# Softmax sums stored in the factors' order, their transpose in the bank of the products with V, and the factors' first DMA issued by ScalarE

## The chip, the cores and the metric

The kernel runs on one NeuronCore of a Trainium2 chip. The metric is the device time of one execution in microseconds; several runs are made and their median is given. The profile is of one more execution of the same program, with its own time.

## What is computed

The reference is attention with a block-causal mask over 8 batches and 8 heads, a gated causal convolution, two dense layers, a two-dimensional Fourier mix and a feed-forward network. What the change touches is the softmax and what follows it:

```python
scores = np.where(mask, scores, -1000000000.0)
scores = scores - np.max(scores, axis=-1, keepdims=True)
attn = np.exp(scores)
attn = attn / (np.sum(attn, axis=-1, keepdims=True) + 1e-09)
return np.matmul(attn, v).astype(np.float32)
...
gate_pre += conv_w[k][None, None, :] * xp[:, k:k + S, :]
gate = 1.0 / (1.0 + np.exp(-gate_pre))
val = x @ w_val
return (gate * val @ w_out).astype(np.float32)
```

There are 8 batches, 8 heads of width 64 and 576 tokens; the kernel works on two heads at a time, so there are 32 pairs of heads, 4 to a batch.

## The kernel before

**Two phases.** `phase1` does the attention of all 32 pairs, with the convolution, the gating, the dense layers and the Fourier transform of each batch woven in as work for TensorE between the attention's steps. `phase2` is the feed-forward network over all tokens. The change is in `phase1`.

**One pair** has 9 units (`i` from 0 to 8): units 0 to 7 are blocks of 128 queries of the two heads by turns (even `i` head 0, odd `i` head 1), unit 8 holds the last 64 queries of both. The main loop counts units over all pairs (`n`), and each step of it emits different stages of different units: the scores `sc` on TensorE (`emit_qk`, L392), the row maximum `mx` on VectorE (`emit_max`), the exponential `PB` on ScalarE (`emit_exp`, L443), the transposes `pt` of `PB` on TensorE (`emit_t`, L490) and their copies out of PSUM, `PTa`, `PTb` and `PTc`, on ScalarE (L512), and at the pair's end the products with V, `av` and `ave` (`emit_av`, L517, matmuls at L535).

**The factors.** The exponential's accumulator leaves each query's sum in a column of the tile `su`: unit `i` writes column `i`, and unit 8, whose scores lie in two tiles, writes columns 8 and 9. `emit_recip` (L454) adds those two, adds 1e-9 and multiplies by 8, and takes three reciprocals into `re`, which re-order the columns: head 0's four blocks, the last block twice, head 1's four blocks. `emit_factors` (L468) transposes `re` on TensorE into a PSUM tile `rt` (L474), and a later stage copies it to SBUF on ScalarE (L479), stores it to a small buffer `f_d` in DRAM (L480) and reads it back by three DMAs that spread each head's factors over 64 partitions of the tile `XF` (L483). `scaled_x` (L548, L549) multiplies `av` and `ave` by `XF`. The rest of `finish_x` makes the high and low parts `XH`, `XL` and the convolution's taps `gate` (L564).

**What sets the order.** The loop's emission order and a scheduler in the framework, which orders each engine's instructions by readiness and priority. Stages that should come later are kept in `Chain` objects: `tick` runs one stage of each live chain per half step, and the list `tq` holds the evacuations of the two PSUM tiles of pool `ps_pt`, so that a new tile of that pool first runs the evacuation before the last. `rt` takes a tile of `ps_pt` before the change. The pool `ps_av` has one tile, `av`. SyncE (SP) issues every DMA of the kernel before the change, in one queue: the loads, the spreads `QQ`, `QD` and `K` of the split queries and keys, `f_d`, `XF` and the stores.

The names of the dense part on TensorE are `psv` (product with w_val), `psx`, `psy` and `pss` (product with w_out and the transforms), all made of matmuls at L165 to L167.

Of the kernel before, what the change touches and what calls it, by code (L numbers as in the profile page):

```python
# [8 lines left out]
F32 = mybir.dt.float32  # L9
F32R = mybir.dt.float32r  # L10
AF = mybir.ActivationFunctionType
ALU = mybir.AluOpType
# [5 lines left out]
def kernel(  # L18
# [13 lines left out]
    nc = tc.nc  # L32
    B, NP, P, S = q.shape
# [68 lines left out]
    def phase1():  # L102
        with ExitStack() as c1:
# [339 lines left out]
            def emit_exp(n):  # L443
                p, i = divmod(n, NB)
                if i == 0:

                    sums[p] = sm.tile([P, 12], F32, tag="su", name="su")
                su = sums[p]
                nm = maxs.pop(n)
                for j, (t, k0, w) in enumerate(scs.pop(n)):  # L450
                    nc.scalar.activation(out=PB[i][:, k0:k0 + w], in_=t, func=AF.Exp, bias=nm,  # L451
                                         accum_out=su[:, i + j:i + j + 1])

            def emit_recip(p):  # L454

                su = sums[p]
                re = sm.tile([P, 10], F32, tag="re", name="re")
                nc.vector.tensor_tensor(out=su[:, 8:9], in0=su[:, 8:9], in1=su[:, 9:10], op=ALU.add)

                nc.vector.tensor_scalar(out=su[:, 0:9], in0=su[:, 0:9], scalar1=1e-9, scalar2=8.0,  # L460
                                        op0=ALU.add, op1=ALU.mult)

                for h in range(2):
                    nc.vector.reciprocal(out=re[:, 6 * h:6 * h + 4], in_=su[:, h:8:2])
                nc.vector.reciprocal(out=re[:, 4:6], in_=su[:, 8:9].to_broadcast([P, 2]))
                recips[p] = re

            def emit_factors(p):  # L468

                re = recips.pop(p)  # L470
                if len(tq) > PTB - 1:
                    tq.pop(0).run()
                ps = ps_pt.tile([P, D], F32, tag="pt", name="rt")
                nc.tensor.transpose(ps[0:10, 0:P], re, ident)  # L474
                rt = sm.tile([P, P], F32, tag="rt", name="rt", bufs=2)
                to, fd = XFS[p % NXF], f_d[p % 2]

                def out():
                    nc.scalar.copy(out=rt[0:10], in_=ps[0:10, 0:P])  # L479
                    nc.sync.dma_start(out=fd, in_=rt[0:10])  # L480
                    row = fd.rearrange("c q -> (c q)").unsqueeze(0)
                    for h, at, n, c in ((0, 0, S, 0), (1, 768, 512, 0), (1, 704, 64, 512)):
                        nc.sync.dma_start(out=to[rs[h], c:c + n], in_=row[:, at:at + n].to_broadcast([64, n]))  # L483
                tq.append(Chain(out))

            tq = []
            VY = 3
            PTB = 2
# [27 lines left out]

            def emit_av(p):  # L517

                if p - 1 in fin:
                    fin[p - 1].run(1)  # L520
                t = ps_av.tile([P, D], F32, tag="av", name="av")
                if len(tq) > PTB - 1:
                    tq.pop(0).run()
# [353 lines left out]
            for n in range(NU + LT + LA):  # L877
# [18 lines left out]
                tick(old)  # L896
                advance(0, n, emit_max, 1)
                advance(1, n, emit_exp)
                old = list(live)
                if 0 <= n - LT < NU:  # L900
                    emit_t(n - LT)
                advance(0, n, emit_max)
                pr, ir = divmod(n - FR, NB)
                if n >= FR and pr < NPAIR:
                    if ir == 0:
                        emit_recip(pr)
                    if ir == 1:
                        emit_factors(pr)
                m = n - LT - LA
                if 0 <= m < NU:  # L910
                    pm, im = divmod(m, NB)
# [11 lines left out]
                            pend.append(dense(pm // NP))  # L923
                step(nst - nst // 2)
                tick(old)
            while pend:
                if not drain[0]:
                    drain[0] = 3
# [276 lines left out]
```

## Time and profile before

| what | value |
|---|---|
| median of 3 runs | 1521.37 us (1520.1 to 1521.79) |
| the profiled execution's own time | 1518.6 us |
| its span, first to last instruction | 1516.8 us |
| mean granted TensorE clock | 0.985 |
| TensorE busy | 1430.2 us (94%) |
| VectorE busy | 831.0 us (55%) |
| ScalarE busy | 648.1 us (43%) |
| GpSimd busy | 302.6 us (20%) |
| DMA queue of SP | 31.5% of 16 engines' span |

Phase 1 takes somewhat less than half the span and phase 2 the rest. The busy shares over the whole span mix the two; a share means something only inside one stage, which the rows further down give. An engine's wait is put down to the instruction that released it last.

### The profile page before, as it was taken

The numbers are of one execution on the slowest core, as the hardware profiler recorded it, in microseconds if no ns is written. First come the engines' busy times: TensorE is split into PE (matmuls) and PEld (weight loads), VectorE is DVE, ScalarE is ACT, GpSimd is POOL, SyncE is SP. The second block draws the span as 40 slices with busy tenths as digits, with TensorE's granted clock in tenths as the row PEclk, the third lists the DMA queues.
The fourth block names the chain that finished last, engine by engine and source line by source line (L and its number), as shares of the span: only waits on it lengthen the run. The fifth ranks groups of instructions, "written<-read, shape, count | busy, mean of one in ns | idle before, by whom it ended". The sixth has DMA issues, their size and how long they took to land.

```text
span 1516.8 us, 23187 instructions
## 1 busy us (share of the span) xinstructions
PE 1430.2 (94%) x8588; PEld 1207.8 (80%) x8588; DVE 831.0 (55%) x1712; ACT 648.1 (43%) x1642; POOL 302.6 (20%) x244
## 2 busy tenths in 40 slices
PE   5688999999999999998999999999999999999998
PEld 3466788888888888986677888888888888888887
DVE  5668687878787878689995223213223222322212
ACT  5577767676767686734452212112121211212110
POOL 2322232323232323122001111011111100111100
PEclk9699999999999999999999999999999999999999
DMA  7566565656565656133441010010101001010000
GB/s 208 150 158 200 132 176 158 167 138 173 137 176 137 176 132 173 46 135 126 168 140 56 0 56 1 1 55 0 56 0 56 1 10 46 1 56 0 29 0 28
DMA packets 122592, 138.75 MB, mean 91 GB/s; under 512 B 24112, under 2 KB 92016, under 8 KB 122480
## 3 DMA queue, kind: packets, MB, share of 16 engines
q1 hardware_dynamic: 122480, 137.27, 31.5%
q8 instruction: 68, 1.11, 0.3%
q14 instruction: 44, 0.36, 0.1%
HBM read 72.05 MB, written 19.04 MB: 60 GB/s over the span
## 4 chain that ended last, share of the span: by engine, by line
PE 50%; DVE 10%; issue 1%; POOL 0%; ACT 0%; DMA 0%; SPq 0%; DVEq 0%; POOLq 0%
PE o L1097 8%; PE psh L1079 8%; PE psh L1078 8%; PE psh L1077 8%; PE o L1095 8%; PE o L1096 8%; DVE st L74 1%; DVE st L76 1%; DVE st L84 1%; DVE st L72 1%; DVE W1L L989 1%; PE av L535 1%; DVE W2L L989 1%; DVE hl L1083 0%; PE pt L506 0%
## 5 line engine op out<-in xcount | busy, mean ns | idle before, releaser
L1083 DVE SCALAR_TENSOR_TENSOR hl<-psh,hh 128x512 fp32r<-128x512 f32 x144 | 99.4, 690 | 397.2 <-ACT hh L1082 397.1
L1082 ACT ACTIVATE hh<-psh 128x512 fp32r<-128x512 f32 x144 | 85.9, 597 | 510.7 <-PE psh L1079 510.7
L1097 PE MATMUL o<-hl,W2H 128*128 128x512 f32 x576 | 220.7, 394 | 13.2 <-DVE hl L1083 13.1
L1079 PE MATMUL psh<-UTH,W1L 128*128 128x512 f32 x576 | 225.4, 391 | 0.9 <-DVE W1L L989 0.9
L1077 PE MATMUL psh<-UTH,W1H 128*128 128x512 f32 x576 | 224.8, 391 | 0.8 <-ACT UTH L1042 0.8
L1078 PE MATMUL psh<-UTL,W1H 128*128 128x512 f32 x576 | 225.0, 391 | 0.4 <-DVE UTL L1043 0.4
L1095 PE MATMUL o<-hh,W2H 128*128 128x512 f32 x576 | 224.1, 389 | 0.0
L1096 PE MATMUL o<-hh,W2L 128*128 128x512 f32 x576 | 224.0, 389 | 0.0
L451 ACT ACTIVATE PB<-sc,mx 128x128 f32<-128x128 f32 (+4 forms) x320 | 165.6, 522 | 39.6 <-DVE mx L438 21.9
L506 PE MATMUL pt<-ident,PB 128*128 128x128 f32 x800 | 142.7, 284 | 17.7 <-ACT PTb L512 7.4
L1097 PEld LDWEIGHTS o<-hl,W2H 128*128 128x128 f32 x576 | 107.6, 189 | 40.9 <-DVE hl L1083 19.2
L506 PEld LDWEIGHTS pt<-ident,PB 128*128 128x128 f32 x800 | 100.4, 144 | 35.0 <-ACT PTb L512 13.5
L1077 PEld LDWEIGHTS psh<-UTH,W1H 128*128 128x128 f32 x576 | 108.6, 189 | 24.0 <-ACT UTH L1042 1.1
L1079 PEld LDWEIGHTS psh<-UTH,W1L 128*128 128x128 f32 x576 | 108.5, 188 | 24.0 <-DVE W1L L989 1.3
L1078 PEld LDWEIGHTS psh<-UTL,W1H 128*128 128x128 f32 x576 | 108.7, 189 | 23.6 <-DVE UTL L1043 0.9
L1095 PEld LDWEIGHTS o<-hh,W2H 128*128 128x128 f32 x576 | 108.1, 188 | 22.8 <-ACT hh L1082 0.2
L1096 PEld LDWEIGHTS o<-hh,W2L 128*128 128x128 f32 x576 | 108.1, 188 | 22.6
L564 DVE SCALAR_TENSOR_TENSOR gate<-XF,cw,gate 128x575 f32<-128x575 f32 (+3 forms) x128 | 123.5, 965 | 2.1 <-ACT gate L63 1.1
L1106 POOL TENSOR_TENSOR U<-o,U 128x512 f32<-128x512 f32 x32 | 40.3, 1290 | 364.8 <-DVE o L1104 364.8
L438 DVE TENSOR_REDUCE mx<-sc 128x1 f32<-128x384 f32 (+2 forms) x192 | 104.4, 561 | 4.9 <-PE sc L167 2.8
L406 PE MATMUL sc<-K,QQ 128*128 128x256 f32 (+2 forms) x256 | 88.6, 356 | 18.6 <-DMA QQ<-QHL 15.4
L560 POOL TENSOR_TENSOR XL<-XF,XH 128x576 fp32r<-128x576 f32 x32 | 45.6, 1426 | 276.7 <-ACT XH L57 268.9
(191 smaller groups left out, 2879.4 us busy)
## 6 DMA issues: line engine op xcount, KB each, us to landing
K<-KP SPq DMA_DIRECT2D x128, 144.0 KB, 2.6
QQ<-QHL SPq DMA_DIRECT2D x128, 128.0 KB, 3.5
rw<-in_w_ch SPq DMA_DIRECT2D x32, 512.0 KB, 4.2
VV<-in_v SPq DMA_DIRECT2D x32, 320.0 KB, 4.3
qraw<-in_q SPq DMA_DIRECT2D x32, 288.0 KB
kraw<-in_k SPq DMA_DIRECT2D x32, 288.0 KB, 5.9
out<-U SPq DMA_DIRECT2D x36, 256.0 KB, 2.0
QQ<-QHL SPq DMA_DIRECT2D x128, 64.0 KB, 2.0
```

The lines of the kernel that those rows point to most:

```text
L406: nc.tensor.matmul(t[:, o:o + w], q[:, 0, m], KK[p][h][:, 0:w], start=True, stop=False)
L438: nc.vector.reduce_max(out=mx[:, j:j + 1], in_=t, axis=AX.X, negate=one)
L451: nc.scalar.activation(out=PB[i][:, k0:k0 + w], in_=t, func=AF.Exp, bias=nm, accum_out=su[:, i + j:i + j + 1])
L506: nc.tensor.transpose(ps[:, j, :], PB[i][:, (j0 + j) * P:(j0 + j + 1) * P], ident)
L564: nc.vector.scalar_tensor_tensor(out=gate[c][:, s:S], in0=XF[:, 0:S - s], scalar=cw[:, c, 4 - s:5 - s], in1=gate[c][:, s:S], op0=ALU.mult, ...
L1077: nc.tensor.matmul(ps, W1H[f][:, c, :], UTH[g][:, c, :], start=(c == 0), stop=False)
L1078: nc.tensor.matmul(ps, W1H[f][:, c, :], UTL[g][:, c, :], start=False, stop=False)
L1079: nc.tensor.matmul(ps, W1L[f][:, c, :], UTH[g][:, c, :], start=False, stop=(c == 3))
L1083: nc.vector.scalar_tensor_tensor(out=l, in0=ps, scalar=0.0, in1=h.bitcast(F32), op0=ALU.max, op1=ALU.subtract)
L1095: nc.tensor.matmul(po[t], W2H[e][:, c], h, start=(e == 0), stop=False)
L1096: nc.tensor.matmul(po[t], W2L[e][:, c], h, start=False, stop=False)
L1097: nc.tensor.matmul(po[t], W2H[e][:, c], l, start=False, stop=(e == NF - 1))
```

## The change

The exponential's sums go straight into the factors' order: columns 0 to 3 head 0, 6 to 9 head 1, and 10 and 11 for unit 8; one add with two columns out makes columns 4 and 5. One reciprocal over ten columns takes the place of three. `emit_recip` is emitted earlier in its step and `emit_factors` at the end of its step. The transpose `rt` is put into the tile of `ps_av` in place of one of `ps_pt`, is no longer in `tq`, and its stage `out` is a chain of its own (`facs`), which `emit_av` runs at the latest. The evacuation of the pair before (`fin[p - 1].run(1)`) is forced in `emit_factors`, no longer in `emit_av`. The store to `f_d` is issued by ScalarE. The loads of `XF` stay with SP.

```diff
+                at = 10 if i == 8 else 6 * (i % 2) + i // 2
...
-                                         accum_out=su[:, i + j:i + j + 1])
+                                         accum_out=su[:, at + j:at + j + 1])
...
-                nc.vector.tensor_tensor(out=su[:, 8:9], in0=su[:, 8:9], in1=su[:, 9:10], op=ALU.add)
-
-                nc.vector.tensor_scalar(out=su[:, 0:9], in0=su[:, 0:9], scalar1=1e-9, scalar2=8.0,
+                nc.vector.tensor_tensor(out=su[:, 4:6], in0=su[:, 10:11].to_broadcast([P, 2]),
+                                        in1=su[:, 11:12].to_broadcast([P, 2]), op=ALU.add)
+
+                nc.vector.tensor_scalar(out=su[:, 0:10], in0=su[:, 0:10], scalar1=1e-9, scalar2=8.0,
                                         op0=ALU.add, op1=ALU.mult)
-                for h in range(2):
-                    nc.vector.reciprocal(out=re[:, 6 * h:6 * h + 4], in_=su[:, h:8:2])
-                nc.vector.reciprocal(out=re[:, 4:6], in_=su[:, 8:9].to_broadcast([P, 2]))
+                nc.vector.reciprocal(out=re, in_=su[:, 0:10])
...
-                if len(tq) > PTB - 1:
-                    tq.pop(0).run()
-                ps = ps_pt.tile([P, D], F32, tag="pt", name="rt")
+                if p - 1 in fin:
+                    fin[p - 1].run(1)
+                ps = ps_av.tile([P, D], F32, tag="av", name="rt")
...
-                    nc.sync.dma_start(out=fd, in_=rt[0:10])
+                    nc.scalar.dma_start(out=fd, in_=rt[0:10])
...
-                tq.append(Chain(out))
+                facs[p] = Chain(out)
...
-                if p - 1 in fin:
-                    fin[p - 1].run(1)
+                facs.pop(p).run()
...
+                pr, ir = divmod(n - FR, NB)
+                if n >= FR and pr < NPAIR and ir == 0:
+                    emit_recip(pr)
                 old = list(live)
...
-                pr, ir = divmod(n - FR, NB)
-                if n >= FR and pr < NPAIR:
-                    if ir == 0:
-                        emit_recip(pr)
-                    if ir == 1:
-                        emit_factors(pr)
...
                 tick(old)
+                if n >= FR and pr < NPAIR and ir == 1:
+                    emit_factors(pr)
```

Three places show what the scheduler makes of it. The first is TensorE's queue in the third pair of a batch (pair 18), once the batches follow one another steadily. `PB_123` and `PB_124` are the probabilities of units 5 and 6, `psx` is the product with w_out.

Before:

```order
L506 MATMUL pt<-ident,PB_123 128x128 x3
L474 MATMUL rt<-ident,re 10x128
L165 MATMUL psx<-GH_158,we_h 128x290
L166 MATMUL psx<-GL_162,we_h 128x290
L167 MATMUL psx<-GH_158,we_l 128x290
L165 MATMUL psx<-GH_159,we_h 128x290
L166 MATMUL psx<-GL_163,we_h 128x290
L167 MATMUL psx<-GH_159,we_l 128x290
L506 MATMUL pt<-ident,PB_124 128x128 x4
```

Now:

```order
L509 MATMUL pt<-ident,PB_123 128x128 x3
L165 MATMUL psx<-GH_158,we_h 128x290
L166 MATMUL psx<-GL_162,we_h 128x290
L167 MATMUL psx<-GH_158,we_l 128x290
L165 MATMUL psx<-GH_159,we_h 128x290
L166 MATMUL psx<-GL_163,we_h 128x290
L167 MATMUL psx<-GH_159,we_l 128x290
L475 MATMUL rt<-ident,re 10x128
L509 MATMUL pt<-ident,PB_124 128x128 x4
```

The transpose of the factors moved behind six matmuls, and nothing else moved. From pair 9 on every pair differs in this alone: in the first and second pair of a batch it moved behind two matmuls of `psv`, in the third behind six of `psx`, in the fourth behind six of `psy`. The number of matmuls is the same.

The second place is SP's queue in pair 1, among the first batches; `QQ_114` and `QQ_116` are the spread queries that the next pair's first scores read.

Before:

```order
L353 DMA QD_113<-QHL 64x2x64 x2
L480 DMA f_d_66<-rt 10x128
L377 DMA QQ_114<-QHL 64x2x256
L379 DMA QQ_114<-QHL 64x256
L377 DMA QQ_116<-QHL 64x2x256
L483 DMA XF_132<-f_d_66 64x576
L483 DMA XF_132<-f_d_66 64x512
L483 DMA XF_132<-f_d_66 64x64
L379 DMA QQ_116<-QHL 64x256
```

Now:

```order
L353 DMA QD_113<-QHL 64x2x64 x2
L485 DMA XF_132<-f_d_66 64x576
L485 DMA XF_132<-f_d_66 64x512
L485 DMA XF_132<-f_d_66 64x64
L377 DMA QQ_114<-QHL 64x2x256
L379 DMA QQ_114<-QHL 64x256
L377 DMA QQ_116<-QHL 64x2x256
```

The store left the queue, and the three loads of `XF` now stand ahead of the spreads `QQ`. So it is in pairs 0 to 7 (in pair 5 with one load between); from pair 8 on at least the first spreads stand ahead of `XF`.

The third place is TensorE's queue in pair 2, where `PB_124` to `PB_126` are units 6 to 8 of the pair and `K_559` or `K_557` the next pair's keys.

Before:

```order
L506 MATMUL pt<-ident,PB_123 128x128 x3
L406 MATMUL sc<-K_559,QQ_114 128x256
L407 MATMUL sc<-KL,QQ_114 128x256
L406 MATMUL sc<-K_559,QQ_114 128x256
L407 MATMUL sc<-KL,QQ_114 128x256
L474 MATMUL rt<-ident,re 10x128
L506 MATMUL pt<-ident,PB_124 128x128 x4
L506 MATMUL pt<-ident,PB_125 128x128 x4
```

Now:

```order
L509 MATMUL pt<-ident,PB_123 128x128 x3
L509 MATMUL pt<-ident,PB_124 128x128 x4
L509 MATMUL pt<-ident,PB_125 128x128 x4
L475 MATMUL rt<-ident,re 10x128
L509 MATMUL pt<-ident,PB_126 128x128 x5
L406 MATMUL sc<-K_557,QQ_114 128x256
L407 MATMUL sc<-KL,QQ_114 128x256
```

The next pair's first scores moved behind the transposes of units 6 to 8, and the factors' transpose stands among these. From the last pair's factors on, the rest of phase 1 and all of phase 2 stand in the same order on every engine as before.

## Rows read from the trace of the kernel before

**Rows 1.** Busy time by stretch of the span: PE, PEld, DVE, ACT, POOL, clock, DMA.

```profile
0.00:200.00 200.00, 154.06 (x1049) 118.62 (x1050) 135.86 (x316) 130.71 (x367) 55.24 (x65) 0.91 0.62 172
200.00:640.00 440.00, 421.99 (x3640) 384.40 (x3640) 348.37 (x874) 321.43 (x931) 126.55 (x92) 1.00 0.55 149
640.00:720.00 80.00, 71.61 (x478) 61.79 (x477) 69.68 (x127) 34.28 (x70) 20.17 (x13) 0.98 0.37 123
720.00:1516.00 796.00, 782.52 (x3427) 642.98 (x3426) 277.06 (x398) 161.71 (x275) 100.61 (x74) 1.00 0.11 37
```

**Rows 2.** Waits of TensorE from 200 to 640 us: total us, times, longest.

```profile
PE rt L474 <- DVE re L465: 14.7, 17, 1.5
PE pt L506 <- ACT PTb L512: 3.2, 5, 0.6
```

**Rows 3.** Waits of TensorE from 0 to 200 us, three of them.

```profile
PE sc L406 <- DMA QQ<-QHL: 15.4, 6, 12.1
...
PE rt L474 <- DVE re L465: 4.9, 5, 2.2
...
PE pt L506 <- ACT rt L479: 2.8, 4, 1.7
```

**Rows 4.** Timeline of TensorE at `rt`: start, us, instruction, [idle before <-releaser].

```profile
355.07 0.27 PE L474 MATMUL rt<-ident,re 128*10 128x128 f32 x1
...
451.64 0.27 PE L474 MATMUL rt<-ident,re 128*10 128x128 f32 x1 [0.59 <-DVE re L465]
...
238.71 0.27 PE L474 MATMUL rt<-ident,re 128*10 128x128 f32 x1 [1.39 <-DVE re L465]
623.47 0.27 PE L474 MATMUL rt<-ident,re 128*10 128x128 f32 x1 [0.24 <-DVE re L465]
...
257.46 0.27 PE L474 MATMUL rt<-ident,re 128*10 128x128 f32 x1 [0.40 <-DVE re L465]
566.30 0.27 PE L474 MATMUL rt<-ident,re 128*10 128x128 f32 x1 [0.30 <-DVE re L465]
```

**Rows 5.** Timeline of TensorE, two matmuls of `psx` that follow each other.

```profile
393.36 0.29 PE L166 MATMUL psx<-GL,we_h 128*128 128x290 f32 x1
393.49 0.29 PE L167 MATMUL psx<-GH,we_l 128*128 128x290 f32 x1
```

**Rows 6.** Timeline of VectorE, the three reciprocals of pair 17.

```profile
374.46 0.24 DVE L464 RECIPROCAL re<-su 128x4 f32<-128x4 f32 x2
374.61 0.14 DVE L465 RECIPROCAL re<-su 128x2 f32<-128x2 f32 x1
```

**Rows 7.** Instructions on tile `su`: duration ns min/median/max, first and last start.

```profile
L464 DVE RECIPROCAL re<-su x64: 133/156/179, 25.7 to 640.1; 128x4 f32<-128x4 f32 x64
L458 DVE TENSOR_TENSOR su<-su x32: 136/160/1115, 24.4 to 639.6; 128x1 f32<-128x1 f32 x32
L460 DVE TENSOR_SCALAR su<-su x32: 153/162/174, 25.5 to 639.8; 128x9 f32<-128x9 f32 x32
```

**Rows 8.** Timeline of VectorE: scaling of `av`, pair 16.

```profile
365.24 0.68 DVE L549 TENSOR_TENSOR XF<-av,XF 128x512 f32<-128x512 f32 x1
```

**Rows 9.** Timeline of SP's queue in pair 1.

```profile
65.65 0.53 SPq L480 DMA_DIRECT2D f_d<-rt  x1
...
68.29 1.83 SPq L483 DMA_DIRECT2D XF<-f_d  x3
```

**Rows 10.** Timelines of TensorE and VectorE behind those DMAs.

```profile
69.02 0.55 PE L406 MATMUL sc<-K,QQ 128*128 128x256 f32 x1 [1.71 <-DMA QQ<-QHL]
...
71.82 0.69 DVE L549 TENSOR_TENSOR XF<-av,XF 128x512 f32<-128x512 f32 x1 [1.63 <-DMA XF<-f_d]
```

**Rows 11.** Instructions on tile `rt`: the store's issue on SP.

```profile
L480 SPq DMA_DIRECT2D f_d<-rt x32: 296/477/572, 44.1 to 641.7; - x32
```

**Rows 12.** Timelines of ScalarE: what follows the copy of `rt`, in two pairs.

```profile
356.14 0.58 ACT L512 COPY PTb<-pt 128x512 f32<-128x512 f32 x1 [0.51 <-PE pt L506]
...
376.32 0.69 ACT L588 ACTIVATE gate<-gate 128x576 f32<-128x576 f32 x1 [0.86 <-DVE gate L564]
```

More of the change, by code (lines that the diff above doesn't have):

```diff
@@ L483, in out @@
                         nc.sync.dma_start(out=to[rs[h], c:c + n], in_=row[:, at:at + n].to_broadcast([64, n]))
-                tq.append(Chain(out))
+                facs[p] = Chain(out)
+            facs = {}
             tq = []
```

## The prediction

> **What bounds the kernel now.** I read the table of busy times by stretch first, since the shares over the whole span mix two phases [rows 1]. From 720 us on TensorE is busy 98% of the time and the change touches nothing there. From 640 to 720 us VectorE has 69.7 of 80 us, and the order of its work is unchanged, so that stretch only moves with what ends before it. From 200 to 640 us TensorE is busy 422.0 of 440 us at full clock, while VectorE has 348.4 and ScalarE 321.4: TensorE is the bound, and what counts there is its 18 us of idle time. Before 200 us no engine is full (TensorE 154 of 200 us, at a clock of 0.91): that stretch is set by chains of waits.
>
> The list of TensorE's waits says what the 18 us are [rows 2]: 14.7 us, in 17 waits, are the transpose of the factors waiting for the reciprocals on VectorE. The next one, 3.2 us, waits for copies of transposed probabilities. In the first 200 us the same wait has 4.9 us in 5, and another 2.8 us are transposes of probabilities that wait for the copy of `rt`, whose PSUM tile they take next [rows 3].
>
> Then the timeline at each transpose of the factors [rows 4]. The 24 pairs from 200 us on fall into four kinds by their place in the batch. First pairs hardly wait (the row at 355.07 shows no idle time). Second pairs wait in all six, 0.59 us at least, and the longest wait of the list, 1.5 us, is one of them. Third pairs wait about 1.3 us, and 1.39 at most, in five cases and 0.24 in the last. Fourth pairs wait 0.30 to 0.40 us in five cases and not in the last. 6 + 6 + 5 are the 17 waits of the list.
>
> **The change part by part.**
>
> *The transpose moves back on TensorE.* The work put ahead of it is the same work that stood behind it, so the wait shrinks by that work's time: matmuls of 290 columns follow each other every 0.13 us [rows 5]. Two of them are 0.26 us (first and second pairs), six are 0.78 us (third pairs). The six of the fourth pairs have 256 columns; by width I estimate 0.69 us.
>
> *One reciprocal for three.* The three take from 374.46 to 374.75 us, 0.29 us [rows 6]. A reciprocal of ten columns is not in the trace. From below the one of four columns bounds it, 0.156 us, from above the three in a row, 0.29. I take 0.16, since `su`'s operation on nine columns takes 0.162 against 0.160 for the add on one column [rows 7]: width counts for little here. So `re` is ready 0.13 us sooner, between 0 and 0.13. The add on two columns I cost as the one on one column, nothing more; once that add took 1.115 us, and the new one may meet the same. The columns that ScalarE's sums go to cost nothing. That the reciprocals are emitted earlier changes nothing from pair 9 on: the instructions between the add and the last reciprocal on VectorE are the same ones in the new order.
>
> *Together, from 200 us on.* Second pairs save 0.26 + 0.13 = 0.39 us each, 2.3 in six. Third pairs save 0.78 + 0.13 = 0.91 us in five and 0.24 in the last, 4.8. Fourth pairs lose their whole wait, 1.6 in five. That is 8.7 of the 14.7 us. The bounds: 14.7 at best, if VectorE also gets to the sums sooner; and at worst about half, 4.4, if TensorE, now earlier at each of them, catches up with VectorE again. I take 8.7: VectorE was released by TensorE's scores or products in between, so that the two start afresh.
>
> *What is late next there.* The 3.2 us of copies stay: they stand at another place in the pair, and the same two tiles are in turn.
>
> *The bank.* `rt` now needs the products of the pair before to have been scaled and taken out of `av`. In steady state that is done some 9 us earlier (the scaling starts at 365.24 [rows 8], the next pair's reciprocals end at 374.75 [rows 6]), so it costs nothing; the cover is gone only in the first pairs, below.
>
> *ScalarE issues the store.* One issue took SP 0.296 to 0.572 us, 0.477 in the middle [rows 11]; no row shows it on ScalarE. All on the path it would be 32 x 0.572 = 18.2 us; from below it is zero, for what SP saves lies on no path from 200 us on. I take zero: behind the copy of `rt` ScalarE waits 0.51 us for TensorE in a first pair and 0.86 us for VectorE in a second [rows 12], and it has 119 of 440 us idle [rows 1]. In the third and fourth pairs the issue stands behind an exponential, ahead of copies that TensorE needs only two transposes later. Queued behind it are those copies, and then the exponentials; if the cover fails, TensorE waits for a free tile of the transposes.
>
> *The first 200 us.* Pairs 0 to 7 have a gain and a loss. The gain is at most the 4.9 us at `rt` and the 2.8 us behind its copy, 7.7 us, since the transposes no longer share a tile with `rt` and `rt` stands behind more of them. The loss: in SP's queue three loads of `XF`, 1.83 us, stand where the store, 0.53 us, stood [rows 9], so the spreads of the queries come 1.3 us later, and the next pair's first scores waited for just these (1.71 us at 69.02) [rows 10]. In seven pairs (1 to 7) that is up to 9.1 us. Against it, TensorE now does the transposes of units 6 to 8 during that time, and `XF` is asked for 2.6 us sooner (65.65 for 68.29), which the scaling waited for [rows 10]. With that `rt`, which now needs the scaling's end, can come at about its old time. Between -7.7 and +9.1 I take -3.0 us: TensorE has other work in the gap, and no engine is full.
>
> *Sum.* 1518.6 - 8.7 - 3.0 + 0 = 1506.9 us, for the profiled execution (span 1516.8 and 1.8 around it). The median of the runs shown is 2.8 us above that execution, 1521.4, so the time to expect is 1509.7 us, 11.7 less. About 0.2%, 3.0 us, is what a measurement of this kernel can tell from no change.
>
> **The rivals.**
>
> *A. The spreads come late.* The loss of 1.3 us in seven pairs comes in full and the gain at `rt` in these pairs not at all: 1521.4 - 8.7 + 9.1 = 1521.8 us, no change. For it: TensorE waits for these spreads six times already, and it is the largest of the waits shown [rows 3], though 12.1 of its 15.4 us are one wait at the program's start. Against it: the transposes that now fill the gap.
>
> *B. ScalarE is held up (slower).* Each issue keeps ScalarE's queue until it is done, the copies out of the two tiles come late, and TensorE waits for a tile in every pair. All of it on the path is 18.2 us: 1521.4 - 11.7 + 18.2 = 1527.9 us. From 0.37 us a pair on the path it uses up the gain, from 0.46 the kernel is slower by more than 0.2%. For it: SP issues much around it, three loads without a gap in 1.83 us for one [rows 9], so that two queues could ask for the same unit at once. Against it: the idle times behind the copy [rows 12]. The Trainium skill, page "Perfetto Trace Analysis", section "DMA Instruction — HWDGE (DVE, Sync)", speaks for this rival: an issuing sequencer first waits out its semaphores, then locks a descriptor generator that others share, and goes on only when all descriptors are made. By that rule the price per issue would be the 0.572 us and a wait behind one of SP's issues of the same size; no run here shows a store issued by ScalarE yet, so the trace neither agrees nor disagrees.
>
> *C. The wait comes back.* TensorE reaches the next factors earlier by what it saved, VectorE does not, and half of the 8.7 us return: 1521.4 - 4.4 - 3.0 = 1514.0 us. For it: in second pairs VectorE works without a break ahead of the reciprocals. Against it: it has 92 of 440 us idle [rows 1].
>
> That the transpose does not move at all is excluded by the order of the instructions.
>
> **How the numbers follow.** The forecast has 0.66 (its own range, from the bounds of its two terms, is 1503 to 1516), C 0.12, A 0.11 and B 0.11. The forecast and C are faster, 0.78; A is no change, 0.11; B is slower, 0.11. The range of 1502 to 1522 us takes in the forecast, C and most of A, and leaves out B and a gain of more than 19 us, which would need both waits at `rt` gone in full.
>
> **What would show it.** In the changed profile TensorE's wait for `re` from 200 us on should fall from 14.7 to about 6 us, nearly all in second and third pairs; the wait for the copy of `rt` should be gone; TensorE's busy time there unchanged at 422 us in a stretch some 9 us shorter. The store should stand on ScalarE's queue with 0.3 to 0.6 us, with no new wait of TensorE for `PTb` beside it. TensorE's waits for `QQ` show rival A: above 15.4 + 5 us I was wrong about the first stretch. Phase 2 should take the same time. The prediction is wrong if the wait for `re` stays above 10 us, if a wait for `PTb` or `PB` grows by more than 5 us, or if the time lies above 1518.

## The result, and the profile after

| | before | changed |
|---|---|---|
| median of 4 runs each, one chip | 1520.73 us (1519.92 to 1521.79) | 1506.78 us (1503.27 to 1509.63) |
| the profiled execution's own time, its span | 1518.6, 1516.8 us | 1509.63, 1507.8 us |
| mean granted TensorE clock in it | 0.985 | 0.980 |

The ratio is 0.9907, with a 95% interval from 0.9884 to 0.9929. On another chip (a_again, among the experiments) the unedited changed kernel gave 1504.12 us against 1522.09, ratio 0.9883 (0.9866 to 0.9900). The change is faster by about 14 us, some 0.9%. The profiled execution of the changed kernel is the longest of its four runs.

Busy time by stretch of the changed kernel, with the columns of [rows 1]; the middle stretches are moved by the 11 us gained until there:

```profile
0.00:200.00 200.00, 156.28 (x1049) 122.76 (x1050) 138.69 (x302) 129.60 (x366) 54.52 (x65) 0.88 0.63 172
200.00:629.00 429.00, 419.78 (x3642) 384.29 (x3641) 345.66 (x827) 319.74 (x933) 127.54 (x92) 1.00 0.57 152
629.00:709.00 80.00, 71.58 (x476) 61.65 (x475) 69.73 (x123) 33.94 (x69) 20.18 (x13) 0.97 0.39 124
709.00:1507.00 798.00, 783.35 (x3427) 643.69 (x3425) 277.79 (x398) 161.81 (x275) 100.10 (x74) 1.00 0.11 36
```

The gain is in the second row: as many matmuls as before (3642 for 3640) in 429 us, and 9.2 us without work in place of 18.0. The first row has a lower clock than before (0.88 for 0.91), the last one is 2 us longer for the same work.

TensorE's waits from 190 to 630 us, beside [rows 2]:

```profile
PE pt L509 <- ACT PTb L515: 3.5, 6, 0.9
PE rt L475 <- DVE re L465: 3.1, 8, 0.9
PE pss L165 <- DVE XA L756: 2.3, 3, 1.1
```

The wait for the reciprocals fell from 14.7 to 3.1 us. The waits for the copies of `PTb` stayed. New is a wait of `pss` for `XA` on VectorE (before, `psv` waited 0.9 us for a tile of that name): this is what is late next.

Timeline at `rt`, beside [rows 4]. Before, in pairs 17 and 18:

```profile
374.90 0.27 PE L474 MATMUL rt<-ident,re 128*10 128x128 f32 x1 [0.76 <-DVE re L465]
...
393.12 0.27 PE L474 MATMUL rt<-ident,re 128*10 128x128 f32 x1 [1.30 <-DVE re L465]
```

Now, in pairs 17, 29, 18 and 19:

```profile
369.06 0.28 PE L475 MATMUL rt<-ident,re 128*10 128x128 f32 x1 [0.19 <-DVE re L465]
...
595.59 0.28 PE L475 MATMUL rt<-ident,re 128*10 128x128 f32 x1 [0.89 <-DVE re L465]
...
386.86 0.28 PE L475 MATMUL rt<-ident,re 128*10 128x128 f32 x1 [0.33 <-DVE re L465]
...
404.95 0.27 PE L475 MATMUL rt<-ident,re 128*10 128x128 f32 x1
```

Third pairs (386.86) wait 0.33 us for 1.30, fourth pairs (404.95) no more. Second pairs wait 0.13 to 0.19 us in four of six; the other two have 0.33 and 0.89. (Waits below 0.15 us are not in the list above.)

The first 200 us, TensorE's waits, beside [rows 3]:

```profile
PE sc L406 <- DMA QQ<-QHL: 12.9, 3, 11.9
PE pt L509 <- ACT PTb L515: 9.6, 13, 1.6
...
PE pt L509 <- ACT PB L452: 4.4, 5, 1.5
...
PE rt L475 <- DVE re L465: 0.4, 1, 0.4
```

The wait for the reciprocals fell from 4.9 to 0.4 us, the transposes' wait for the copy of `rt` (2.8) is gone, and a part of that for `QQ` too. In their place TensorE waits for ScalarE: for `PTb` 9.6 us, 4.2 before.

VectorE's chain in pair 17, to be compared with [rows 6, 7]:

```profile
366.58 0.14 DVE L460 TENSOR_TENSOR su<-su 128x2 f32<-128x2 f32 x1
366.63 0.81 DVE L566 SCALAR_TENSOR_TENSOR gate<-XF,cw,gate 128x573 f32<-128x573 f32 x1
...
368.05 0.17 DVE L463 TENSOR_SCALAR su<-su 128x10 f32<-128x10 f32 x1
368.12 0.76 DVE L627 TENSOR_TENSOR GL<-GF,GH 128x580 fp32r<-128x580 f32 x1
368.80 0.21 DVE L465 RECIPROCAL re<-su 128x10 f32<-128x10 f32 x1
```

One reciprocal takes 0.21 us. It stands 2.2 us behind the add, because work of other chains stands between: the chain's own instructions take 0.5 us.

ScalarE's store, as a group of the instructions on its tile, beside [rows 11] (ACTq is ScalarE's queue of DMAs):

```profile
L482 ACTq DMA_DIRECT2D f_d<-rt x32: 279/280/551, 26.9 to 630.8; - x32
```

Its surroundings in ScalarE's timeline in pair 18, beside [rows 12]:

```profile
388.44 0.47 ACT L452 ACTIVATE PB<-sc,mx 128x256 f32<-128x256 f32 x1 [0.17 <-DVE mx L430]
388.50 0.28 ACTq L482 DMA_DIRECT2D f_d<-rt  x1
...
388.90 0.58 ACT L515 COPY PTb<-pt 128x512 f32<-128x512 f32 x1
389.37 0.49 ACT L452 ACTIVATE PB<-sc,mx 128x256 f32<-128x256 f32 x1
...
389.83 0.59 ACT L515 COPY PTb<-pt 128x512 f32<-128x512 f32 x1
```

The issue lies under the exponential. From that exponential's start to the next copy it is 0.46 us, and 0.46 us again for the next one, which has no issue beside it: the store costs ScalarE nothing here.

TensorE's queue has one more move, which the section on the change does not have: from pair 9 on not every pair differs in the place of `rt` alone. In the fourth pair of five batches two matmuls of scores stood ahead of seven of `psy` and now stand behind them. The first of the nine matmuls and the transpose behind the last, before and now, in one of these pairs:

```profile
340.10 0.48 PE L406 MATMUL sc<-K,QQ 128*128 128x512 f32 x1
...
341.83 0.33 PE L506 MATMUL pt<-ident,PB 128*128 128x128 f32 x1
```

```profile
335.02 0.36 PE L165 MATMUL psy<-dft,XEEH 128*128 128x258 f32 x1
...
336.41 0.33 PE L509 MATMUL pt<-ident,PB 128*128 128x128 f32 x1
```

The nine take 1.73 us from start to start in the old order and 1.39 in the new one (1.39 to 1.45 in the five), without idle time in the record in either: 1.6 us in the five batches that no wait shows. The move comes with that of `rt`: e4 has the new order, e2, e3 and e8 the old one with its 1.73 us.

### The profile page after: what moved, and what is told of

Read it like the earlier page. It is cut to its first block, busy times and chain, and to the rows that moved or that the text cites. A ratio compares the mean times of both kernels' runs of the same rounds, so it can differ in the third digit from the quotient of the medians.

```text
span 1507.8 us, 22996 instructions
## 1 busy us (share of the span) xinstructions
PE 1431.0 (95%) x8588; PEld 1212.4 (80%) x8588; DVE 831.9 (55%) x1648; ACT 645.1 (43%) x1642; POOL 302.3 (20%) x244
## 4 chain that ended last, share of the span: by engine, by line
PE 74%; DVE 13%; DMA 4%; ACT 4%; issue 2%; POOL 2%; SPq 1%; DVEq 0%; ACTq 0%; POOLq 0%
PE o L1098 8%; PE psh L1080 8%; PE psh L1078 8%; PE psh L1079 8%; PE o L1096 8%; PE o L1097 8%; PE av L537 5%; PE pt L509 4%; PE sc L406 2%; PE sc L407 2%; POOL XA L772 2%; ACT PB L452 2%; PE psx L165 2%; PE psx L166 1%; PE psx L167 1%
## 5 line engine op out<-in xcount | busy, mean ns | idle before, releaser
L1098 PE MATMUL o<-hl,W2H 128*128 128x512 f32 x576 | 220.7, 394 | 14.4 <-DVE hl L1084 14.3
L406 PE MATMUL sc<-K,QQ 128*128 128x256 f32 (+2 forms) x256 | 89.8, 360 | 16.0 <-DMA QQ<-QHL 12.9
```

Source lines behind the costliest of these rows:

```text
L406: nc.tensor.matmul(t[:, o:o + w], q[:, 0, m], KK[p][h][:, 0:w], start=True, stop=False)
L1098: nc.tensor.matmul(po[t], W2H[e][:, c], l, start=False, stop=(e == NF - 1))
```

## The experiments

Two lengths are taken from every trace: from the first scores of pair 0 to those of pair 9 (12.08 and 193.61 us in the kernel before), and from there to those of pair 31 (618.84). "Idle" is TensorE's idle time in it. "Low" is the time in the first 200 us with TensorE's clock at 1.2 GHz, the lower of its two levels. The idle time at `rt` takes in waits below 0.15 us, which the lists of waits leave out. The lengths and idle times of a row come from one trace, the median from all its runs. A pair's time in the text is that from its first scores to those of the next pair.

| kernel | to pair 9: us, idle, low | pairs 9 to 31: us, idle, of it at `rt` | median, us | ratio to before, 95% |
|---|---|---|---|---|
| before | 181.5, 32.8, 37.5 | 425.2, 18.7, 14.6 | 1520.73 | |
| changed | 182.9, 31.7, 47.7 | 413.1, 9.2, 3.5 | 1506.78 | 0.9907 |
| a_again | 177.8, 32.4, 34.0 | 412.6, 8.5, 3.3 | 1504.12 | 0.9883 (0.9866, 0.9900) |
| e1_sp_store | 181.5, 32.1, 41.0 | 416.2, 9.9, 6.0 | 1510.63 | 0.9925 (0.9913, 0.9937) |
| e2_act_store | 179.1, 35.4, 37.5 | 423.2, 16.8, 13.0 | 1514.77 | 0.9961 (0.9948, 0.9973) |
| e3_recip | 180.4, 30.5, 37.5 | 425.4, 17.8, 14.2 | 1521.86 | 0.9998 (0.9986, 1.001) |
| e4_move | 179.4, 30.7, 37.5 | 421.0, 13.3, 6.9 | 1510.76 | 0.9917 (0.9905, 0.993) |
| e5_move_store | 178.4, 32.1, 34.1 | 415.0, 10.5, 4.1 | 1508.76 | 0.9918 (0.9901, 0.9936) |
| e6_twice | 185.0, 33.0, 47.7 | 419.2, 12.2, 7.9 | 1515.27 | 0.9958 (0.9944, 0.9972) |
| e7_early_sp | 182.1, 30.5, 44.4 | 416.2, 9.9, 4.7 | 1507.21 | 0.9898 (0.9880, 0.9917) |
| e8_short_only | 184.4, 32.9, 51.1 | 422.4, 14.3, 5.5 | 1517.13 | 0.9967 (0.9955, 0.9979) |
| v1_short | 175.1, 32.2, 27.2 | 411.0, 4.7, 0 | 1501.25 | 0.9863 (0.9844, 0.9881) |
| v1_again | 178.8, 33.5, 34.0 | 411.8, 5.5, 0 | 1504.05 | 0.9881 (0.9864, 0.9898) |
| v2_loads | 181.0, 32.1, 40.9 | 413.0, 5.2, 0 | 1507.08 | 0.9898 (0.9881, 0.9916) |

The runs came in three groups, each on a chip of its own with runs of the kernel before beside it: e1 to e4 (1521.76 us), a_again, e6, e7 and v1_short (1522.09), and e5, e8, v1_again and v2 (1522.31).

### The change in parts: e1 to e4

**e1, the changed kernel with SP's store:**

```diff
-                    nc.scalar.dma_start(out=fd, in_=rt[0:10])
+                    nc.sync.dma_start(out=fd, in_=rt[0:10])
```

> The changed kernel with one edit taken back: the store of the factors to the small DRAM buffer is issued by SP again. Theory 1 (place of the transpose): the gain is TensorE's wait for the reciprocals, which from 200 us on fell from 14.7 to about 3 us because matmuls now stand ahead of the factors' transpose; the issuer of the store is worth nothing there. Then this run stays near the changed kernel's 1506.8 us (1503 to 1510), the wait for the reciprocals from 190 to 630 us stays near 3 us, and only the first 200 us may differ. Theory 2 (the queue): the gain comes with the store's leaving SP's queue; then most of the 13.9 us is lost again and the time is 1515 us or more. Theory 3 (fewer reciprocals) says the same of this run as theory 1.

Measured 1510.63 us, just past theory 1's range. In pairs 9 to 31 it takes 3.1 us more than the changed kernel, and the wait at `rt` is 6.0 us for 3.5. So the issuer seems to be worth something there (e7 below takes a part of this back), though most of the gain stays without it: theory 2 falls as the main cause and theory 1 as the only one. VectorE's timeline in pair 13 shows where the 0.88 us of TensorE's wait come from:

```profile
293.45 0.16 DVE L460 TENSOR_TENSOR su<-su 128x2 f32<-128x2 f32 x1 [0.74 <-ACT PB L452]
...
295.70 0.21 DVE L465 RECIPROCAL re<-su 128x10 f32<-128x10 f32 x1
```

VectorE stands idle ahead of the add, since the last exponential is late. The exponential stands behind `QHL`, the split of the next queries, in ScalarE's queue, and that waits for DMAs of SP's queue. The split in front of this exponential, in e1 and in the changed kernel:

```profile
291.77 0.69 ACT L345 ACTIVATE QHL<-qraw 128x576 fp32r<-128x576 f32 x1 [1.43 <-DMA K<-KP]
```

```profile
290.20 0.69 ACT L345 ACTIVATE QHL<-qraw 128x576 fp32r<-128x576 f32 x1 [0.24 <-DMA QQ<-QHL]
```

The waits for DMAs ahead of `QHL` on ScalarE from 200 to 630 us in e1 (`u_d` and `K` are neighbours of `QQ` in SP's queue), and VectorE's wait behind them:

```profile
ACT QHL L345 <- DMA QQ<-QHL: 6.5, 7, 1.9
ACT QHL L345 <- DMA u_d<-XA: 1.7, 2, 1.1
ACT QHL L345 <- DMA K<-KP: 1.4, 1, 1.4
```

```profile
DVE su L460 <- ACT PB L452: 2.6, 4, 1.0
```

The same in the changed kernel:

```profile
ACT QHL L345 <- DMA QQ<-QHL: 2.5, 4, 0.9
ACT QHL L345 <- DMA K<-KP: 1.4, 1, 1.4
ACT QHL L345 <- issue: 0.3, 1, 0.3
```

```profile
DVE su L460 <- ACT PB L452: 0.7, 1, 0.7
```

9.6 us of waits with SP's store, 4.2 with ScalarE's, of which 0.3 without a known releaser (the kernel before had 5.6). The traces of e4 and e6, which have a store on SP's queue, show 9.9 and 9.8 us; a_again, e5 and e7, with ScalarE's store in these pairs, 4.1 to 5.2. This is a second path to `rt`: SP's queue, split, exponential, sums, reciprocals.

**e2, the kernel before with ScalarE's store** (the same line, the other way round):

> The kernel before with one edit: ScalarE issues the store of the factors. Theory 1 (place of the transpose): the 17 waits for the reciprocals from 200 us on stay at about 14.7 us, so that stretch keeps its length; the first 200 us may move by a few us either way; 1518 to 1523 us. Theory 2 (the queue): 1512 us or less, since the store was what held the first pairs and the spreads back. The rival of the prediction that ScalarE is held up by the issue would show as a time above 1523 us with new waits of TensorE for the copies out of the transposes.

1514.77 us: between the theories. The wait at `rt` stays (13.0 us), as theory 1 has it, but pairs 9 to 31 take 2.1 us less and the first nine pairs 2.4 less at the same low-clock time. The ratio, 0.9961, is clear of 1. There was hardly a new wait for copies out of the transposes (`pt` for `PTb`: 3.0 us in the first 200 us and 3.9 after, 4.2 and 3.2 before): the rival that ScalarE is held up is out.

**e3, the kernel before with the new sums and one reciprocal** (the parts of the diff in `emit_exp` and `emit_recip` alone):

> The kernel before with one edit: the sums in the factors' order and one reciprocal of ten columns in place of three; the transpose keeps its place and its bank, SP keeps the store. Theory 1 (place of the transpose): VectorE is done 0.07 to 0.16 us sooner in each of the 17 pairs in which TensorE waits from 200 us on, so 1.2 to 2.7 us: 1518.0 to 1519.5 us, and the wait for the reciprocals falls from 14.7 to between 12 and 13.5 us. Theory 3 (fewer reciprocals carry the gain, because VectorE gets ahead by more than their own time): 1512 us or less, and the wait falls below 8 us.

1521.86 us, no difference, and 425.4 us in pairs 9 to 31: by itself this part is worth nothing that can be measured. The wait at `rt` fell by 0.08 us in each third and fourth pair (1.30 to 1.22, 0.32 to 0.24), but in second pairs, where the exponential is late in some, the waits rose from 6.3 to 6.7 us in sum. Theory 3 falls, and theory 1's 1.2 to 2.7 us did not come either.

**e4, the changed kernel with the old sums, three reciprocals and SP's store:** the place and the bank of the transpose are left (no run has the one without the other).

> The changed kernel with the sums, the three reciprocals and SP's store as before: what is left is the transpose's place in the order and its bank. Theory 1 (place of the transpose): most of the gain stays; the changed kernel's 1506.8 us plus 0.16 us in the pairs that still wait (about 12 of 24), so 1507 to 1511 us, and the wait for the reciprocals from 190 to 630 us between 4 and 7 us. Theory 3 (fewer reciprocals): 1515 us or more, with a wait above 10 us.

1510.76 us, inside theory 1's range, and a wait of 6.9 us at `rt`, at the edge of it: by the medians the move alone brings 11.0 us. In the trace pairs 9 to 31 take only 4.3 us less, though the wait at `rt` fell by 7.7: VectorE waits 4.0 us for exponentials and ScalarE 9.9 us for SP's DMAs, so TensorE ran into what was late next. This trace is of the longest of e4's five executions, 1513.93 us; the shortest took 1506.75.

### The store and SP's queue: e5, e6, e7

**e5, e4 with ScalarE's store:**

> The changed kernel with the sums and the three reciprocals of before: the transpose's new place and bank together with ScalarE's store, all but the single reciprocal. The move alone took 4.3 us out of pairs 9 to 31, the move with the single reciprocal 9.1, all three 12.1 and 12.6. Theory 1 (the single reciprocal is worth its own 0.1 us a pair in the pairs that still wait): pairs 9 to 31 take 9 to 11 us less than before and TensorE's wait for the reciprocals there is 4 to 6 us. Theory 2 (the single reciprocal carries what the move alone did not bring): 4 to 6 us less, with a wait of 6 us or more.

10.2 us less in pairs 9 to 31, and a wait of 4.0 us: theory 1. By the traces, with the 12.1 and 12.6 of the two of the whole change, the single reciprocal is worth about 2 us there, once move and store have been made, and the store on top of the move 6.0 us (421.0 to 415.0). The medians do not bear out the second figure: e4 has 0.9917 of the time before and e5 0.9918. e4's trace is of the longest of its five executions and e5's of the shortest of its six (1505.93 to 1512.52 us). By the medians the move brings most of the gain; neither the store (e5) nor the single reciprocal (e1, 0.9925) alone adds to it, and only both together do (0.9907 and 0.9883, of which the first still overlaps with e4 and e5).

**e6, the changed kernel with a second, unread store by SP:**

```diff
                     nc.scalar.dma_start(out=fd, in_=rt[0:10])
+                    nc.sync.dma_start(out=f_x[p % 2], in_=rt[0:10])
```

> The changed kernel with one addition: SP also stores the factors, to a buffer that nobody reads, so that SP's queue has the issue again that the change took from it, while the factors still go out early through ScalarE. In the run with SP's store alone the wait for the reciprocals was 6.1 us in pairs 9 to 31 against 3.5, and ScalarE's split of the queries waited 9.6 us for DMAs against 4.2. Theory A (the work in SP's queue): both come back, 5 to 7 us and 8 to 10 us, and the time is like that run's, 1509 to 1512 us. Theory B (only the factors' early arrival counts): the time stays at the changed kernel's 1505 to 1508 us and the waits at 3 to 4 and 4 to 5 us.

1515.27 us, beyond theory A's range and 11 us slower than the changed kernel beside it (a_again, 1504.12). ScalarE's waits for SP's DMAs from 200 to 630 us are 9.8 us again, with 5.5 for `QQ`, and VectorE's for the exponential 3.2:

```profile
ACT QHL L346 <- DMA QQ<-QHL: 5.5, 6, 1.6
```

```profile
DVE su L461 <- ACT PB L453: 3.2, 4, 1.0
```

The factors went out as early as in the changed kernel (0.03 us behind the copy of `rt` in the middle, in both; 0.83 in e1), so it is SP's queue that counts: the work on it, the one more DMA, or the store's own wait in the queue for the copy of `rt`, which no run here separates. The 22 issues of 0.48 us in the middle, as in [rows 11], are 10.5 us of SP's time; pairs 9 to 31 took 6.1 and 6.6 us more than in the two traces of the change. The Trainium skill, page "Trainium Kernel Development and Optimization", section "Key Constraints", says that DMAs of several issuing engines run on the same 16 DMA engines and that issuing from several saves the sequencer's issue time alone. What e6 lost is within that issue time, so the trace agrees with the rule as far as it goes.

**e7, the changed kernel with SP's store in pairs 0 to 7:**

```diff
-                    nc.scalar.dma_start(out=fd, in_=rt[0:10])
+                    (nc.sync if p < 8 else nc.scalar).dma_start(out=fd, in_=rt[0:10])
```

> The changed kernel with SP issuing the store in pairs 0 to 7 and ScalarE from pair 8 on. TensorE's order in the first stretch is then that of the run with SP's store, the rest that of the changed kernel. Theory A (the spreads stand behind the loads of the factors in SP's queue, and this costs the first stretch 3 us): the first scores of pair 8 come 3 to 4 us sooner than in the changed kernel, pairs 9 to 31 keep their gain of 12 us, and the time is 1502 to 1505 us. Theory B (the loss is the clock's chance): the same time as the changed kernel beside it, within 1 us, and low-clock time that differs without pattern.

1507.21 us, nothing gained on a_again's 1504.12: theory A falls. (The first scores of pair 8 came 3.3 us sooner than in the first trace of the changed kernel, but 2.0 later than in a_again's.) That the spreads stand behind the loads of `XF` in the changed kernel costs nothing visible.

The run also says how far e1 can be trusted. From pair 8 on ScalarE issues e7's store, and yet its pairs 9 to 31 take 416.2 us, as long as in e1. 1.9 of the 3.1 us lost against the changed kernel lie in pairs 9 and 10, where `rt` of pair 9 waits 1.43 us (0.13 in the changed kernel), and 1.3 in pair 24. e1 loses 2.1 of its 3.1 us in pairs 9 and 10 too, with a wait of 1.36 us at the same `rt`. So these come with SP's store in the first pairs, and from pair 11 on e1 lies only 0.9 and 1.4 us above the two traces of the change, no more than e7 does (1.2 and 1.7). That SP's store in the later pairs costs time is shown by e6 (5.7 and 6.2 us from pair 11 on), not by e1.

### The first stretch: a_again

> The changed kernel itself, unedited, for a second trace of it and a median beside the other runs of this chip. In its first trace the first scores of pair 8 came 2.7 us later than in the kernel before, with 10.2 us more at TensorE's lower clock in the first 200 us, and pairs 9 to 31 took 12.1 us less. If the clock of the first stretch is chance of an execution, this trace shows another sum of low-clock time there (37 us as before, or any other) and the time moves with it; if it comes from the order of the work, the sum is about 48 us again and pair 8 is again 2 to 4 us late. Pairs 9 to 31 should again take 11 to 13 us less.

The same program took 182.9 us to pair 9 in one execution and 177.8 in the other, with nearly the same idle time (31.7 and 32.4). What differs is the clock. The first 190 us of before, of the changed kernel and of a_again, columns as in [rows 1]:

```profile
0.00:190.00 190.00, 144.98 (x981) 110.30 (x982) 127.14 (x297) 123.63 (x347) 52.24 (x63) 0.90 0.61 169
```

```profile
0.00:190.00 190.00, 146.28 (x966) 113.40 (x968) 129.89 (x281) 122.98 (x347) 51.67 (x63) 0.87 0.62 170
```

```profile
0.00:190.00 190.00, 146.02 (x1014) 113.99 (x1015) 135.06 (x292) 126.40 (x356) 53.15 (x64) 0.91 0.65 176
```

About as many microseconds of busy TensorE did 966 matmuls at a mean clock of 0.87 and 1014 at 0.91. 13.7 us more at 1.2 GHz went with 5.1 us more until pair 9. In the table the idle time of this stretch stays between 30.5 and 35.4 us in all 14 traces, and its length goes with the low-clock time: 175.1 us at 27.2, 185.0 at 47.7. So the change did neither what I hoped here (3.0 us gained) nor what its rival feared (9.1 lost), and the chance of an execution is larger than the gain that I hoped for. Why the clock differs between executions stays open. Pairs 9 to 31 repeat within 0.5 us here, and within 0.8 us in v1; each of the other kernels has one trace only.

### A shorter chain: v1, e8, v2

**v1, on top of the change** (it leaves out the 1e-9 on all sums but those of unit 8):

```diff
-                nc.vector.tensor_tensor(out=su[:, 4:6], in0=su[:, 10:11].to_broadcast([P, 2]),
-                                        in1=su[:, 11:12].to_broadcast([P, 2]), op=ALU.add)
-                nc.vector.tensor_scalar(out=su[:, 0:10], in0=su[:, 0:10], scalar1=1e-9, scalar2=8.0,
-                                        op0=ALU.add, op1=ALU.mult)
+                nc.vector.tensor_scalar(out=su[:, 4:6], in0=su[:, 10:11].to_broadcast([P, 2]), scalar1=su[:, 11:12],
+                                        scalar2=1e-9, op0=ALU.add, op1=ALU.add)
...
-                    nc.scalar.copy(out=rt[0:10], in_=ps[0:10, 0:P])
+                    nc.scalar.activation(out=rt[0:10], in_=ps[0:10, 0:P], func=AF.Copy, scale=0.125)
```

> The changed kernel with a shorter chain on VectorE: one operation makes the two columns of unit 8, the 1e-9 on the other columns is left out (the sums are at least 1), and the factor 8 moves to ScalarE's copy of the transposed factors. VectorE then has the add, one foreign operation and the reciprocal where it had two and two. What the transposes still wait for in pairs 9 to 31 is 3.5 us. If that wait is VectorE's chain, it falls below 1 us and the time by 2 to 4 us against the changed kernel beside it; if it is ScalarE's late exponential, about half of it stays and the time falls by less than 2 us.

> The version with the short chain on top of the change, unedited, for a second trace and beside the next run: pairs 9 to 31 take 14 us less than in the kernel before, no wait at the transpose, 1498 to 1504 us by what the clock grants in the first stretch.

VectorE's chain in pair 17 of v1_short:

```profile
360.21 0.23 DVE L460 TENSOR_SCALAR su<-su 128x2 f32<-128x2 f32 x1 [0.76 <-ACT PB L452]
...
361.04 0.20 DVE L462 RECIPROCAL re<-su 128x10 f32<-128x10 f32 x1
```

TensorE's waits from 190 to 630 us in it:

```profile
PE pt L506 <- ACT PTb L512: 3.4, 6, 0.9
PE psv L165 <- DVE gv L614: 0.3, 1, 0.3
...
```

The reciprocal starts 0.83 us behind the sums, for 2.22; no wait at `rt` is left, even in this pair, where the exponential was late by 0.76. Pairs 9 to 31 take 411.0 and 411.8 us, about 1.4 less than the two traces of the change: the chain was what the rest of the wait was for, but it was worth less than I expected. 1501.25 and 1504.05 us are faster than before beyond doubt; against the change (1504.12 beside the first) the intervals overlap, so that only the traces show this last step.

**e8, the short chain in the kernel before, without move and store:**

> The kernel before with the short chain on VectorE alone (one operation for unit 8's two columns, one reciprocal, the factor 8 in ScalarE's copy of the transposed factors, the 1e-9 left out of the other columns): the transpose keeps its place, SP keeps the store. If the time from the sums to the reciprocals is what TensorE waits for, this removes the second foreign operation from the chain (0.4 to 0.75 us), so the 14.6 us of waits at the transpose fall to 5 to 9 us and pairs 9 to 31 take 5 to 9 us less than before, without any move: 1513 to 1517 us. If instead ScalarE's exponential or SP's queue is late next, the waits fall by less than 4 us and the time stays at 1518 us or more.

Between the two: 1517.13 us, a ratio of 0.9967, and 2.9 us less in pairs 9 to 31. From 200 to 630 us TensorE no longer waits for the reciprocals, but for a tile:

```profile
PE pt L502 <- ACT PTb L508: 8.0, 16, 0.7
PE rt L470 <- ACT PTb L508: 5.0, 8, 1.7
```

`rt` and the transposes share two tiles there, and once the reciprocals are early `rt` waits for a copy of `PTb`. That is what the bank of `av` is good for: in v1, which has the new bank and the new place, `rt` takes none of these tiles, and the same chain meets no such wait.

**v2, v1 with ScalarE issuing the loads of the raw queries and keys from pair 10 on** (`nc.scalar if p > 9 else nc.sync` in `load`):

> The short-chain version with one addition: from pair 10 on ScalarE also issues the two loads of the raw queries and keys, so that SP's queue has two issues fewer in each pair. Theory A (SP's queue is late: a DMA more on it cost 6 us in pairs 9 to 31): ScalarE's split of the queries waits less than in the version without it (3.6 to 5 us), VectorE's sums wait less for the exponential, and pairs 9 to 31 take 1 to 3 us less. Theory B (the queue has slack again once the store is gone, or ScalarE's own issues now cost as much): within 1 us, or slower with new waits of TensorE for ScalarE's copies.

Theory B: 413.0 us in pairs 9 to 31, against 411.0 and 411.8. ScalarE's split waits less (2.7 us for 5.1 and 4.1 in v1), yet nothing is gained by it. Either SP's queue is no longer what TensorE waits for once the store is gone, or ScalarE's own issues take back what it saves; this run does not tell.

## Why the prediction was right, and where not

The forecast was 1509.7 us, 2.9 above the median measured and inside its range. For the profiled execution 1506.9 was forecast and 1509.63 came: pairs 9 to 31 gave 12.1 us where 8.7 were forecast, the first stretch lost 1.4 where 3.0 were to be gained, and from pair 31 to the end 2.0 were lost where nothing was forecast: 1518.6 - 12.1 + 1.4 + 2.0 = 1509.9, and 0.2 were gained ahead of the first scores. That the sum came so near is in part luck: the terms were off by 3.4 us one way and by 4.4 and 2.0 the other. Two figures of the working are wrong, without weight in the forecast: 32 x 0.572 is 18.3, not 18.2, and the bounds given for the two terms make a range of 1499 to 1526 us, not of 1503 to 1516.

- **The move on TensorE: right.** Third pairs went from 1.30 to 0.33 us (0.97, forecast 0.91), fourth pairs lost their wait. Second pairs, where the waits before differ most, lost 4.4 us in sum (6.3 to 1.8) where 2.3 were forecast; e1, with SP's store, lost 2.6 there (to 3.7). e4 shows that the move by itself brings 11.0 us by the medians. The move of the scores behind `psy`, 1.6 us, stood in no term.
- **One reciprocal: mis-sized, with the right effect.** It takes 0.208 us, not 0.16. In pair 17 `rt` starts 0.05 us behind its recorded end, though, where it was 0.15.
- **"What SP saves lies on no path from 200 us on": this step failed.** Zero was right for ScalarE and wrong for SP. I followed the factors' own path and not SP's queue to the split of the queries and the exponential. e6 shows it: a store more on SP's queue costs 11 us by the medians. What the store's leaving is worth in the change itself stays open: by single traces 2.1 us alone, 3.1 in the whole change and 6.0 on top of the move in pairs 9 to 31, but e7 has the 3.1 without SP's store in the later pairs, and the medians of e4 and e5 do not show the 6.0. In e4's trace half of the gain went back, as rival C has it, though by a late exponential; by its median it did not.
- **The bank: right** in steady state. e8 shows more than I had said: a shared tile would have been the next wait.
- **What is late next: half right.** The waits for `PTb` stayed (3.2, now 3.5 us), but the 2.3 us for `XA` were not foreseen.
- **The first 200 us: wrong.** 1.4 us lost, 3.0 forecast as a gain. The waits at `rt` and for its copy fell as forecast, by 7.3 us in sum, and came back as waits for ScalarE; the transposes of units 6 to 8 now follow each other without scores between them, which is the likely reason. The wait for `PTb` grew by 5.4 us, which I had named as a sign that the prediction is wrong. It is not rival B: e1 and e4, with SP's store, have 10.8 and 11.5 us there, and e2, with ScalarE's store and the old order, 3.0. Rival A's sign, a longer wait for `QQ`, did not come either (12.9 for 15.4).
- **Phase 2: not the same time.** The order of the work is the same, but 1.6 of the 2.0 us lost are one fall of the clock (below).
- **ScalarE held up (B): did not come.** By the rule of the Trainium skill, page "Perfetto Trace Analysis", section "DMA Instruction — HWDGE (DVE, Sync)", on which this rival drew, I had put an issue at up to the 0.572 us of SP's rows. The traces show 0.28 us in the middle and 0.55 at most, in pair 18 beside a running instruction, with no copy later for it.

## What to carry to other kernels

Where a busy engine waits at one instruction for a chain on another, moving independent work ahead of it pays until the next late input of that chain shows; so follow every input of the chain back, the queues of DMAs included, before pricing an issue at zero. Count the foreign instructions that a scheduler puts between the links of a short chain: in pair 17 dropping a link of 0.17 us shortened the chain from 2.22 to 0.83 us. Split the time by stretch before judging an edit, since a wavering clock in one stretch hides a gain in another. But a trace is one execution: where one kernel's trace is of its longest run and the other's of its shortest, as in e4 and e5, hold the stretch against the medians before giving a part its price.

## What the runs showed of the hardware

The lower clock also came in phase 2, in some executions. In the changed kernel it fell for 3.4 us behind an idle time of 2.12 us of TensorE. The stretch around it, and the matmul behind the idle time:

```profile
786.40:793.40 7.00, 4.89 (x14) 3.88 (x15) 7.00 (x13) 2.47 (x4) 0.00 (x0) 0.76 0.00 0
...
788.51 0.73 PE L1098 MATMUL o<-hl,W2H 128*128 128x512 f32 x2 [2.12 <-DVE hl L1084]
```

The same place in the kernel before, 10.6 us later:

```profile
797.00:804.00 7.00, 4.88 (x21) 4.05 (x22) 7.00 (x13) 3.06 (x6) 0.00 (x0) 1.00 0.00 0
...
799.12 0.74 PE L1097 MATMUL o<-hl,W2H 128*128 128x512 f32 x2 [2.13 <-DVE hl L1083]
```

The idle time is the same and the clock stayed, so that 21 matmuls stand against 14. Across this place the lead over the kernel before shrinks from 10.6 to 9.0 us. Why the clock falls in one execution and not in the other stays open.

A wait of TensorE cost more than its idle time in the record. Pairs 16, 20, 24 and 28 of the changed kernel are the same 166 matmuls in the same order, at a granted clock of 1.00, the higher level. They took 18.74 us without idle time, 19.29 with one wait of 0.43 us, 19.60 with one of 0.76 and 19.94 with one of 1.09: 0.10 to 0.12 us on top of each wait. That matmuls in a row start every 0.13 us though each lasts 0.29 [rows 5] would make it 0.16, the overlap that the first one behind a wait loses.

Between pairs 9 and 31 the idle time fell by 9.4 us and the length by 12.1. Six waits fewer at `rt` explain 0.6 to 1 us of the difference (an estimate, with 0.10 to 0.16 each), and the scores moved behind `psy` 1.6 us.
